# Two attention blocks, forward and backward: the DMA issues of GpSimd moved onto SyncE's queue in a written order

## The chip, the core and the metric

One core of a Trainium2 chip. The metric is the device time of one execution in microseconds (us); of several runs the median is given. Engines: PE (TensorE matmuls), PEld (its weight loads), DVE (VectorE), ACT (ScalarE), POOL (GpSimd), SP (SyncE, which only issues transfers here).

## The reference

Two independent attention blocks A and B with cached keys and values, their outputs side by side, and the gradients of all ten inputs for a given `grad_out`. All arrays are bf16. For each block:

```
B, Sq, D = 8, 96, 640;  H, Sk, Dh = 32, 512, 128
q = (x @ wq) in heads                     # [8, 32, 96, 128]
scores = einsum("bhqd,bhkd->bhqk", q, k_cache) * Dh**-0.5
p = softmax(scores)
o = einsum("bhqk,bhkd->bhqd", p, v_cache)
out = o in rows [8, 96, 4096] @ wo        # [8, 96, 640]
# and by the chain rule: dx, dk_cache, dv_cache, dwq, dwo
```

The bulk of the traffic is k_cache and v_cache (33.6 MB each per block) and their gradients, as large.

## The kernel before, in words

The kernel is one stream of ticks. A tick is one batch element b of one head h of one block; a head has 8 ticks, a block 256, and block B follows A without a break. Each step of the work is a Python closure handed to an emitter with a tick and a slot (`em.add(tick, slot, fn)`, L21); the emitter sorts by tick, then slot, and calls them, so that the order of the program is that of the sorted list. A scheduler behind it may move instructions of an engine past each other; those wrapped in `pinned` (L111) stay in program order on their engine. Slots (L51) put transfers at LOAD = 0, the first of a tick, and the attention steps between 5 and 54; head work is at 90, group work at 95.

For a tick ct the steps lie at fixed distances (`OFF`, L45): K is loaded 5 ticks ahead, V 3 ahead; K is transposed either by PE (`c_s1`, L285) or, for every second pair of batch elements of most heads, by a DMA transpose (`c_xt`, L275) 3 ahead; V is always transposed by a DMA transpose at ct itself. All of these are on SP. Loads and transposes are for a pair of batch elements: 256 KB, `NB = 2`. Then come the scores S (L298), their maximum on DVE (L300), the exponential on ACT (L310), the normalised P on POOL (L329) at ct+3, the transposed P (L365) and dV (L389, evicted by ACT at L392) at ct+4, O (L359) and the product O x dO on POOL (L407) at ct+5, dP and its row term dl (L417, L419) and dS on DVE (L421) at ct+6, the transposed dS (L346) and dK (L432, evicted by ACT at L435) at ct+7, dQ (L340) at ct+8. L340 is the last that reads K, L417 the last that reads the transposed V. K has 7 buffers, V 5, the transposed V 4, the transposed K 2.

Per head there is also: loading wq for two heads (`pA`, L190; 320 KB) and wo (`pA2`, L199; 160 KB) some ten ticks ahead, their transposes, the projections of Q and dO (L243), and behind the head the gradients dwo (`qB`, L470) and dwq for two heads (`qD`, L490). Every five or six heads (a group) the output rows and dx rows are accumulated in SBUF (`gU`, L512); at the last group they are written out. At the change of block, x and grad_out of block B are loaded in 12 row tiles `ld_tmp` (L118) and transposed on PE (L134), and loaded again in natural layout (L144).

Transfers are issued from two engines:
- SP: K and V loads, DMA transposes, x and grad_out. Only the `ld_tmp` loads are pinned; the order of the rest is the scheduler's.
- POOL, between its products: the stores of dV and dK (`c_st`, L398; 256 KB each, one of each for a pair, at the end of a tick: slot 54.3), the weights (slot 54.6), dwo (L474) and dwq (L496) as soon as their last part is evicted, and the output and dx rows of block A (L543). For the last head of B and its rows, SP issues these.

The eviction buffers of dV and dK are three each; dwo and dwq have one each.

Of the kernel before, what the change touches and what calls it, by code (L numbers as in the profile page):

```python
# [53 lines left out]
def build_block(tc, em, tick0, blk, x, kc, vc, wq, wo, g_all, out_all, dx, dk, dv, dwq, dwo, ident, ones, pools, HG=6, first=True, groups=None):  # L54
    nc = tc.nc
# [206 lines left out]
    def c_ld(h, b, n, bufs):  # L262
        def f():
            src = kc if n == "K" else vc
            X = kvp.tile([128, NB, KC, 128], BF16, name=n + "_sb", bufs=bufs)
            nc.sync.dma_start(X[:], src[b:b + NB, h].rearrange("b (p c) d -> p b c d", c=KC))
            for i in range(NB):
                st = CS.setdefault((blk, h, b + i), {})
                st[n + "_sb"], st[n + "_all"] = X[:, i], X
        return f  # L270

    def c_xt(h, b, name, bufs):
        def f():
            XT = kvp.tile([128, NB * KC, 128], BF16, name=name, bufs=bufs)
            nc.sync.dma_start_transpose(XT[:], CS[(blk, h, b)][name[0] + "_all"][:].rearrange("p a c d -> p (a c d)"))  # L275
# [119 lines left out]
    def c_st(h, b, which):  # L395
        def f():
            dst = dv if which == "v" else dk
            pinned(nc.gpsimd.dma_start(dst[b - 1:b + 1, h].rearrange("b (p c) d -> p b (c d)", c=KC), SB.pop((blk, h, b // 2, which))[:]))  # L398
        return f
# [59 lines left out]
    def qB(h, di):  # L459
        def f():  # L460
            st = HS[(blk, h)]
            Onat = st["Onat"]
            if "dwo_sb" not in st:
                st["dwo_sb"] = hd.tile([128, D], BF16, name="dwo_sb", bufs=1)
                st["dwo_n"] = 0
            dwo_sb = st["dwo_sb"]
# [4 lines left out]
            evac(EV["qB%d" % di], dwo_sb[:, c0:c0 + w], w_ps[:])  # L471
            st["dwo_n"] += 1
            if st["dwo_n"] == len(wsplits):
                (nc.gpsimd if first or h < H - 1 else nc.sync).dma_start(dwo[h * 128:(h + 1) * 128, :], dwo_sb[:])  # L474
        return f

    def qD(h, c_lo, c_hi):
        def f():
            st = HS[(blk, h)]
            dQnat = st["dQnat"]  # L480
            if "dwq_sb" not in st:
                st["dwq_sb"] = hd.tile([128, DC, 256], BF16, name="dwq_sb", bufs=1)
                st["dwq_n"] = 0
            dwq_sb = st["dwq_sb"]
# [7 lines left out]
            evac(EV["qD"], dwq_sb[:, c_lo:c_hi, :].rearrange("p a b -> p (a b)"), w_ps[:, 0:ncn * 256], scale)  # L492
            st["dwq_n"] += ncn
            if st["dwq_n"] == DC:
                with nc.allow_non_contiguous_dma(reason="dwq slice of two heads"):
                    (nc.gpsimd if first or h < H - 1 else nc.sync).dma_start(dwq_v[:, :, (h - 1) * 128:(h + 1) * 128], dwq_sb[:])  # L496
        return f
# [3 lines left out]
    def gU(g, which, t, gi):  # L501
        def f():
# [39 lines left out]
            if gi == len(gsplits) - 1:  # L542
                (nc.gpsimd if first else nc.sync).dma_start(dst_flat[t * 128:(t + 1) * 128, :], ob)  # L543
        return f
# [7 lines left out]
    for g in range(NG):  # L552
        h0 = GH0[g]
        for hh in range(groups[g]):
            h = h0 + hh
            c0t = tick0 + h * B
            if not (first and h == 0):
                em.add(c0t + HK["pA"], 54.6, pA(h))
                em.add(c0t + HK["pA2"], 54.6, pA2(h))
            em.add(c0t + HK["pB"], SL_HEAD, pB(h))  # L560
# [11 lines left out]
            for b in range(B):  # L572
# [169 lines left out]
```

## Time and profile before

| | before |
|---|---|
| runs | 1705.34, 1693.32, 1706.98 us |
| median | 1705.34 us |
| span of the profiled execution | 1699.8 us, granted PE clock 0.998 |
| time of the profiled execution | not told by the page; the span is 5.5 us under the median |
| PE, DVE, ACT, POOL busy | 99, 78, 83, 61% of the span |
| DMA issues | 927 on SP (378 of them transposes), 713 on POOL |
| moved by DMA | 423 MB, mean 249 GB/s |

How to read it: the span is from the first to the last instruction of one execution. A matmul's end is modelled, and matmuls overlap, so PE's busy share tells where it stood still and not how near it is to its peak. A row of a wait view says which instruction waited, what ended the wait (`<-`), and then the total in us, the number of waits and the longest. In rows of instructions `x256 | 195.0, 762 | 9.1` is count, busy us, mean ns of one, and the engine's idle us before them. `SPq` is SP's instruction queue. The time to landing of a DMA runs from its issue to the last of its bytes.

### The profile page before, as it was taken

Reading aid. Unit: us, or ns where it says so; the run is one execution under the profiler, and the core shown is the slowest. Engines: PE = TensorE matmul, PEld = TensorE weight load, DVE = VectorE, ACT = ScalarE, POOL = GpSimd, SP = SyncE. Lnnn points to the kernel's source line nnn. Section 1 sums busy time; section 2 is a strip of 40 time slices with the busy share of each in tenths; the row PEclk is TensorE's granted clock in tenths of the full one; section 3 lists DMA queues with packets and bytes.
Section 4 is the critical chain, followed back from the end, with each engine's and each line's share of the span. In section 5 each row is a group of like instructions: output and inputs, shape, how many; then the busy total and the mean of one; then the engine's idle time right before and its main releaser. Section 6 shows DMA issues by size and latency. Waiting matters only on the chain.

```text
span 1699.8 us, 56567 instructions
## 1 busy us (share of the span) xinstructions
PE 1675.7 (99%) x22024; PEld 1343.8 (79%) x22024; DVE 1329.8 (78%) x3052; ACT 1405.2 (83%) x3518; POOL 1040.3 (61%) x1747
## 2 busy tenths in 40 slices
PE   8999999999999999999999999999999999999999
PEld 7877778778778778777778877887788778778876
DVE  6887678878788878787778876787788778878877
ACT  6998889869869869878768998897799679878975
POOL 3676567646647647656566764675576557656754
PEclk9999999999999999999999999999999999999999
DMA  9999999999999999999999999999899989999994
GB/s 256 252 259 250 258 225 260 262 242 243 262 221 252 268 238 259 225 251 237 281 256 269 273 270 248 238 289 248 218 261 276 237 221 261 281 217 240 263 247 141
DMA packets 600429, 423.05 MB, mean 249 GB/s; under 512 B 419360, under 2 KB 557984, under 8 KB 600160
## 3 DMA queue, kind: packets, MB, share of 16 engines
q1 hardware_dynamic: 546576, 242.08, 72.2%
q0 software_dynamic: 53584, 177.35, 32.7%
q8 instruction: 173, 2.83, 0.7%
q14 instruction: 96, 0.79, 0.2%
HBM read 161.09 MB, written 159.12 MB: 188 GB/s over the span
## 4 chain that ended last, share of the span: by engine, by line
PE 89%; DMA 4%; ACT 3%; issue 1%; DVE 1%; POOL 0%; SPq 0%; DVEq 0%; ACTq 0%; POOLq 0%
PE q_ps L243 12%; PE o_ps L512 12%; PE dwo_ps L470 6%; PE dV_ps L389 6%; PE dK_ps L432 6%; PE S_ps L298 6%; PE dP_ps L417 6%; PE dwq_ps L490 6%; PE x_ps L340 5%; PE x_ps L365 5%; PE dst_ps L346 5%; PE x_ps L359 5%; PE kT_ps L285 3%; PE n_ps L258 3%; PE nat_ps L455 2%; DMA VT<-V_sb 1%
## 5 line engine op out<-in xcount | busy, mean ns | idle before, releaser
L329 POOL TENSOR_SCALAR P_sb<-E_sb,rinv 96x512 bf16<-96x512 bf16 x512 | 352.6, 689 | 567.8 <-DVE rinv L320 559.2
L310 ACT ACTIVATE E_sb<-S_ps,negm 96x512 bf16<-96x512 f32 x512 | 351.0, 686 | 187.6 <-DVE negm L300 181.9
L421 DVE SCALAR_TENSOR_TENSOR dS_sb<-dP_ps,dl_ps,P_sb 96x512 bf16<-96x512 f32 x512 | 382.1, 746 | 60.9 <-PE dl_ps L419 54.6
L300 DVE TENSOR_REDUCE negm<-S_ps 96x1 f32<-96x512 f32 x512 | 347.6, 679 | 50.9 <-PE S_ps L298 46.6
L435 ACT ACTIVATE dK_sb<-dK_ps 128x512 bf16<-128x512 f32 x512 | 302.1, 590 | 63.4 <-PE dK_ps L432 56.5
L392 ACT ACTIVATE dV_sb<-dV_ps 128x512 bf16<-128x512 f32 x512 | 311.6, 609 | 0.0
L378 ACT ACTIVATE PT_sb<-x_ps 128x384 bf16<-128x384 bf16 x512 | 253.1, 494 | 0.0
L512 PEld LDWEIGHTS <-OD 128*128 128x128 bf16 x1536 | 132.2, 98 | 100.4 <-issue 1.0
L398 POOL DMA_DIRECT2D out_dram<-dV_sb x256 | 194.9, 761 | 11.8 <-issue 8.6
L398 POOL DMA_DIRECT2D out_dram<-dK_sb x256 | 195.0, 762 | 9.1 <-issue 4.4
L389 PE MATMUL dV_ps<-dOnat_h,P_sb 96*128 96x128 bf16 x2048 | 198.2, 219 | 0.8 <-DVE dOnat_h L160 0.6
L417 PE MATMUL dP_ps<-VT,dOT_h 128*96 128x512 bf16 x512 | 195.4, 382 | 3.0 <-DMA VT<-V_sb 3.0
L432 PE MATMUL dK_ps<-Qnat_h,dS_sb 96*128 96x128 bf16 x2048 | 198.1, 219 | 0.1
L407 POOL TENSOR_TENSOR prod<-OD,dOT_h 128x96 bf16<-128x96 bf16 x512 | 184.2, 360 | 13.8 <-ACT OD L375 12.6
L348 DVE COPY dST_sb<-dst_ps 128x384 bf16<-128x384 bf16 x512 | 177.1, 346 | 10.5 <-PE dst_ps L346 10.3
L365 PE MATMUL x_ps<-ident,P_sb 96*128 96x96 bf16 x2048 | 172.0, 205 | 0.8 <-POOL P_sb L329 0.3
L359 PE MATMUL x_ps<-PT_sb,V_sb 128*128 128x96 bf16 x2048 | 172.3, 206 | 0.2 <-ACT PT_sb L378 0.2
L346 PE MATMUL dst_ps<-ident,dS_sb 96*128 96x96 bf16 x2048 | 172.3, 206 | 0.2 <-DVE dS_sb L421 0.2
L340 PE MATMUL x_ps<-dST_sb,K_sb 128*128 128x96 bf16 x2048 | 171.0, 206 | 1.3 <-ACT dK_sb L435 0.8
L375 ACT ACTIVATE OD<-x_ps 128x192 bf16<-128x192 f32 (+1 forms) x515 | 167.9, 326 | 3.9 <-PE x_ps L340 3.9
L320 DVE RECIPROCAL rinv<-rowsum 96x1 f32<-96x1 f32 x512 | 79.9, 156 | 106.0 <-ACT E_sb L310 100.4
L340 PEld LDWEIGHTS <-K_sb 128*128 128x128 bf16 x2048 | 131.1, 98 | 25.1 <-issue 1.6
(84 smaller groups left out, 3744.4 us busy)
## 6 DMA issues: line engine op xcount, KB each, us to landing
out_dram<-dV_sb POOLq DMA_DIRECT2D x256, 256.0 KB, 5.2
out_dram<-dK_sb POOLq DMA_DIRECT2D x256, 256.0 KB, 5.3
K_sb<-in_A_k_cache_dram SPq DMA_DIRECT2D x128, 256.0 KB, 5.3
V_sb<-in_A_v_cache_dram SPq DMA_DIRECT2D x128, 256.0 KB, 5.2
K_sb<-in_B_k_cache_dram SPq DMA_DIRECT2D x128, 256.0 KB, 5.0
V_sb<-in_B_v_cache_dram SPq DMA_DIRECT2D x128, 256.0 KB, 4.9
out_dram<-dwo_sb POOLq DMA_DIRECT2D x63, 160.0 KB, 4.8
out_dram<-dwq_sb POOLq DMA_DIRECT2D x31, 320.0 KB, 6.1
```

The source lines that it names most:

```text
L300: nc.vector.tensor_reduce(negm[:], S_ps[:], axis=AX.X, op=ALU.max, negate=True)
L310: nc.scalar.activation(E_sb[:], st["S_ps"][:], ACT.Exp, bias=st["negm"][:], scale=1.0, accum_out=rowsum[:])
L329: pinned(nc.gpsimd.tensor_scalar(P_sb[:], st["E_sb"][:], st["rinv"][:], 0.0, op0=ALU.mult, op1=ALU.add))
L340: nc.tensor.matmul(dQT_ps, st["K_sb"][:, c, :], st["dST_sb"][:, c * Sq:(c + 1) * Sq], start=(c == 0), stop=(c == KC - 1))
L389: nc.tensor.matmul(dV_ps[:, c * 128:(c + 1) * 128], P_sb[:, c * 128:(c + 1) * 128], hs["dOnat_h"][:, b * 128:(b + 1) * 128], start=True, s ...
L392: nc.scalar.activation(SB[(blk, h, b // 2, "v")][:, b % 2], dV_ps[:], ACT.Identity, scale=1.0)
L398: pinned(nc.gpsimd.dma_start(dst[b - 1:b + 1, h].rearrange("b (p c) d -> p b (c d)", c=KC), SB.pop((blk, h, b // 2, which))[:]))
L417: nc.tensor.matmul(dP_ps[:], hs["dOT_h"][:, tok], st["VT"], start=True, stop=True)
L421: nc.vector.scalar_tensor_tensor(dS_sb[:], dP_ps[:], dl_ps[:, 0:1], st["P_sb"][:], op0=ALU.subtract, op1=ALU.mult)
L432: nc.tensor.matmul(dK_ps[:, c * 128:(c + 1) * 128], dS_sb[:, c * 128:(c + 1) * 128], hs["Qnat_h"][:, b * 128:(b + 1) * 128], start=True, s ...
L435: nc.scalar.activation(SB[(blk, h, b // 2, "k")][:, b % 2], dK_ps[:], ACT.Identity, scale=1.0)
L512: nc.tensor.matmul(o_ps[:], src[:, t * 128:(t + 1) * 128], rhs, start=(hh == 0), stop=(hh == groups[g] - 1))
```

## The change

All 713 issues on POOL move to SP. There the K and V loads, the DMA transposes, the stores and the weights are now pinned, in a written order; the first weights and the loads in natural layout are not. Within a tick SP's order is: loads (slot 0), transposes (1), the stores of dV and dK (1.5), dwo, dwq and rows (1.6), weights (1.7). The stores of dV and dK keep their tick, one behind the eviction, but stand at the beginning of that tick and no longer at its end. The stores of dwo, dwq, the output rows and dx rows become steps of their own (`qB_st`, `qD_st`, `gU_st`), one tick behind their last product. The weights keep their ticks, ten and nine ahead of their head. The first wo load goes to SP too, and is not pinned.

In the built program PE, DVE and ACT have the same sequence of instructions as before, and POOL the same but for the DMAs. For a pair SP's order becomes V load, K load, K transpose (every second pair), dK store, V transpose, dV store.

```diff
@@ pA, pA2
-                        pinned(nc.gpsimd.dma_start(wq_p[:], wq_v[:, :, h * 128:(h + 2) * 128]))
+                        pinned(nc.sync.dma_start(wq_p[:], wq_v[:, :, h * 128:(h + 2) * 128]))
...
-            ld = nc.gpsimd.dma_start(wo_h[:], wo[h * 128:(h + 1) * 128, :])
+            ld = nc.sync.dma_start(wo_h[:], wo[h * 128:(h + 1) * 128, :])
@@ c_ld, c_xt
-            nc.sync.dma_start(X[:], src[b:b + NB, h].rearrange("b (p c) d -> p b c d", c=KC))
+            pinned(nc.sync.dma_start(X[:], src[b:b + NB, h].rearrange("b (p c) d -> p b c d", c=KC)))
...
-            nc.sync.dma_start_transpose(XT[:], CS[(blk, h, b)][name[0] + "_all"][:].rearrange("p a c d -> p (a c d)"))
+            pinned(nc.sync.dma_start_transpose(XT[:], CS[(blk, h, b)][name[0] + "_all"][:].rearrange("p a c d -> p (a c d)")))
@@ c_st
-            pinned(nc.gpsimd.dma_start(dst[b - 1:b + 1, h].rearrange("b (p c) d -> p b (c d)", c=KC), SB.pop((blk, h, b // 2, which))[:]))
+            pinned(nc.sync.dma_start(dst[b - 1:b + 1, h].rearrange("b (p c) d -> p b (c d)", c=KC), SB.pop((blk, h, b // 2, which))[:]))
@@ qB, qD, gU
+    def qB_st(h):
+        def f():
+            pinned(nc.sync.dma_start(dwo[h * 128:(h + 1) * 128, :], HS[(blk, h)]["dwo_sb"][:]))
...
+    def qD_st(h):
+        def f():
+            with nc.allow_non_contiguous_dma(reason="dwq slice of two heads"):
+                pinned(nc.sync.dma_start(dwq_v[:, :, (h - 1) * 128:(h + 1) * 128], HS[(blk, h)]["dwq_sb"][:]))
...
+    def gU_st(which, t):
+        def f():
+            dst_flat = out_flat if which == 0 else dx_flat
+            pinned(nc.sync.dma_start(dst_flat[t * 128:(t + 1) * 128, :], S.pop(("ob", which, t))))
@@ build_block
-                em.add(c0t + HK["pA"], 54.6, pA(h))
-                em.add(c0t + HK["pA2"], 54.6, pA2(h))
+                em.add(c0t + HK["pA"], SLOTS["LOAD"] + 1.7, pA(h))
+                em.add(c0t + HK["pA2"], SLOTS["LOAD"] + 1.7, pA2(h))
...
-                    em.add(ct + OFF["s4"] + 1, 54.3, c_st(h, b, "v"))
-                    em.add(ct + OFF["s7"] + 1, 54.3, c_st(h, b, "k"))
+                    em.add(ct + OFF["s4"] + 1, SLOTS["LOAD"] + 1.5, c_st(h, b, "v"))
+                    em.add(ct + OFF["s7"] + 1, SLOTS["LOAD"] + 1.5, c_st(h, b, "k"))
...
+            em.add(c0t + hk["qB"][-1] + 1, SLOTS["LOAD"] + 1.6, qB_st(h))
...
+            if h % 2 == 1:
+                em.add(c0t + hk["qD"][-1][0] + 1, SLOTS["LOAD"] + 1.6, qD_st(h))
...
+            if g == NG - 1 and gi == len(gsplits) - 1:
+                em.add(tk + 1, SLOTS["LOAD"] + 1.6, gU_st(which, t))
```

More of the change, by code (lines that the diff above doesn't have):

```diff
@@ L464, in f @@
                 st["dwo_sb"] = hd.tile([128, D], BF16, name="dwo_sb", bufs=1)
-                st["dwo_n"] = 0
             dwo_sb = st["dwo_sb"]
@@ L471, in f @@
             evac(EV["qB%d" % di], dwo_sb[:, c0:c0 + w], w_ps[:])
-            st["dwo_n"] += 1
-            if st["dwo_n"] == len(wsplits):
-                (nc.gpsimd if first or h < H - 1 else nc.sync).dma_start(dwo[h * 128:(h + 1) * 128, :], dwo_sb[:])
+        return f
+    def qB_st(h):
+        def f():
+            pinned(nc.sync.dma_start(dwo[h * 128:(h + 1) * 128, :], HS[(blk, h)]["dwo_sb"][:]))
         return f
@@ L482, in f @@
                 st["dwq_sb"] = hd.tile([128, DC, 256], BF16, name="dwq_sb", bufs=1)
-                st["dwq_n"] = 0
             dwq_sb = st["dwq_sb"]
@@ L492, in f @@
             evac(EV["qD"], dwq_sb[:, c_lo:c_hi, :].rearrange("p a b -> p (a b)"), w_ps[:, 0:ncn * 256], scale)
[L493 to L496, printed above, removed]
+        return f
+    def qD_st(h):
+        def f():
+            with nc.allow_non_contiguous_dma(reason="dwq slice of two heads"):
+                pinned(nc.sync.dma_start(dwq_v[:, :, (h - 1) * 128:(h + 1) * 128], HS[(blk, h)]["dwq_sb"][:]))
         return f
@@ L542, in f @@
             if gi == len(gsplits) - 1:
-                (nc.gpsimd if first else nc.sync).dma_start(dst_flat[t * 128:(t + 1) * 128, :], ob)
+                S[("ob", which, t)] = ob
+        return f
+    def gU_st(which, t):
+        def f():
+            dst_flat = out_flat if which == 0 else dx_flat
+            pinned(nc.sync.dma_start(dst_flat[t * 128:(t + 1) * 128, :], S.pop(("ob", which, t))))
         return f
```

## The prediction

> **What bounds the kernel now.** I read four views in this order: the page's busy times and chain, PE's waits, the DMA queues, and the rows of the engines that issue DMAs.
>
> ```profile
> PE 1675.7 (99%) x22024; PEld 1343.8 (79%) x22024; DVE 1329.8 (78%) x3052; ACT 1405.2 (83%) x3518; POOL 1040.3 (61%) x1747
> ...
> PE 89%; DMA 4%; ACT 3%; issue 1%; DVE 1%; POOL 0%; SPq 0%; DVEq 0%; ACTq 0%; POOLq 0%
> ```
>
> PE has 99% of the span and 89% of the chain that ended last. Busy time is no peak, so I checked it by the starts of successive matmuls in the trace: 42 ns apart at 96 columns, 56 at 128, 110 at 256, 135 at 320, 216 at 512, that is columns/2.4 + 2 ns. Over all 22,024 matmuls this sums to 1618 us. Of the span of 1699.8 us only 82 us are left, 5 of them before the first and after the last matmul, and some 20 at the hand-over behind each of the 512 one-column dl_ps matmuls. The change leaves PE's order untouched (the built programs of both kernels have the same sequence on PE, DVE and ACT). So what it can win is the part of PE's stalls that DMAs cause. PE's waits, and ACT's one:
>
> ```profile
> PE dP_ps L417 <- DMA VT<-V_sb: 3.0, 2, 2.4
> PE tp_ps L134 <- DMA ld_tmp<-in_grad_out_dram: 2.7, 1, 2.7
> PE S_ps L298 <- DMA KT<-K_sb: 2.1, 1, 2.1
> PE kT_ps L285 <- ACT dK_sb L435: 1.6, 1, 1.6
> ...
> PE tp_ps L134 <- DMA ld_tmp<-in_B_x_dram: 0.9, 1, 0.9
> ```
>
> ```profile
> ACT dK_sb L435 <- DMA out_dram<-dK_sb: 3.1, 2, 1.8
> ```
>
> Each row: us in total, times, longest. They are few and long: late transposes of V and K, late loads for the change of block, and twice an eviction of dK that has no free buffer since an earlier dK store has not landed. A long one costs twice, by the clock:
>
> ```profile
> 826.00:829.00 3.00, 0.26 (x3) 0.16 (x3) 0.00 (x0) 0.86 (x2) 0.88 (x2) 1.00 1.02 367
> 829.00:832.00 3.00, 3.00 (x35) 2.67 (x34) 1.75 (x5) 1.86 (x5) 0.81 (x2) 0.62 1.30 283
> ```
>
> In the windows view (us; PE, PEld, DVE, ACT, POOL busy; granted clock; DMA share; GB/s) PE stands still at 826 to 829 us, and then runs at a mean clock of 0.62. The clock records show half rate for 3.4 us, twice in the span: after this stall and after the one at 123 us.
>
> Why are those transfers late? SP stands in its own way:
>
> ```profile
> SPq L275 <- DMA K_sb<-in_A_k_cache_dram: 169.4, 57, 9.0
> SPq L275 <- DMA K_sb<-in_B_k_cache_dram: 152.0, 61, 4.8
> ```
>
> 118 of the 122 K transposes wait on SP for the load of their K: in the trace 119 of them are issued only two places behind it. The wait is 2.7 us on average, and all loads and transposes behind it wait too; then they leave in a burst.
>
> ```profile
> q1 hardware_dynamic: 546576, 242.08, 72.2%
> q0 software_dynamic: 53584, 177.35, 32.7%
> ```
>
> These are packets, MB, and packet time as a share of 16 engines: q1 is SP's queue, q0 POOL's. Together 105%: with both at work, packets wait for each other.
>
> **The change part by part.** The tick is 3.24 us (first L417 matmul at 23.3, last at 1679.5 us, 511 steps), a pair of ticks 6.48 us.
>
> POOL loses 713 issues (256+256 stores of dV and dK, 63 dwo, 31 dwq, 64 wo, 31 wq, 12 output rows).
>
> ```profile
> L398 POOL DMA_DIRECT2D out_dram<-dK_sb x256 | 195.0, 762 | 9.1 <-issue 4.4
> L398 POOL DMA_DIRECT2D out_dram<-dV_sb x256 | 194.9, 761 | 11.8 <-issue 8.6
> ```
>
> With the smaller groups 525 us of its 1040 go. POOL is not the bound: it waits 559 us for rinv. Ten PE stalls end with P_sb; only at 278.0 and 516.4 us did a POOL issue directly precede the late P_sb, 0.28 and 0.24 us. Gain 0.5 us (bounds 0 and all ten, 2.5).
>
> SP gains these 713. Its prices:
>
> ```profile
> L266 SPq DMA_DIRECT2D K_sb<-in_A_k_cache_dram x128: 367/478/1639, 2.4 to 814.3; - x128
> ```
>
> ```profile
> L275 SPq DMA_TRANSPOSE VT<-V_sb x256: 1231/1440/6143, 12.2 to 1656.9; - x128
> ```
>
> (ns, min/median/max.) No 256 KB store is issued by SP before; the nearest row is the K load, equal in bytes. By the minima, 1262 plain DMAs x 0.37 + 378 transposes x 1.23 = 932 us, 55% of the span. By the means of the trace (362.7 us / 549 = 0.66 and 600.1 / 378 = 1.59) 1434 us, 84%, or 5.6 of the 6.48 us of a pair. Both fit. I take nearer the minima, since the long ones stand in bursts behind other transfers.
>
> The waits that come in. The order on SP is now, for a pair, V load, K load, K transpose (every second pair), dK store, V transpose, dV store. The K load waits for PE's L340 matmul of its tick (seven buffers), as before. A dK store waits for ACT's eviction of the tick before, and behind it on SP stand the V transpose, the dV store and the next loads. In the timeline a dK matmul at 802.15 us is evicted by 803.75, and the next tick's L340, which the K load ahead of the store needs, starts at 804.77: the product is there a microsecond early. The dV store has a tick of its own in the same way. Cost nothing; if ACT ran more than that late, the V transposes would be late next, with 11.9 us between landing and use in the median of the trace (5% under 2.7). In return the K transpose now stands 6 or 8 places behind its K load in 116 of 122 cases: the 321 us of waits above go, and the bursts.
>
> In both built programs eight landing semaphores go round on SP's queue, so each DMA waits for the eighth before it to land. There were 927 DMAs, 3.6 a pair, eight of them 14.3 us; now 1640, 6.4 a pair, eight of them 8.1 us. Landings took 5.2 us (K loads) to 6.1 (V transposes) in the median, 8.5 and 10.2 at 95%. So this wait is new in the tail; a landing late by 2 us is covered by the 11.9.
>
> The DMA engines. In the packet records the median 256-byte packet of a transpose takes 18 ns (mean 31), 1,024 bytes of a load 46 (53), and POOL's packets of 4,096 bytes 165 (204). By the medians all traffic takes 1281 us of 16 engines, 75%. On SP's queue the stores leave in 1,024, 1,280 and 512-byte packets (46, 55, 27 ns): 377 + 61 + 67 = 505 us in place of 445, in all 1341 us, 79%: 5.24 us of a pair. The other end, with the means (72.2% of the span, and 505 x 53/46 = 577), is 1804 us, 106%. I take the medians, as the means hold the wait for the other queue's packet, which is no more.
>
> Two rules of the Trainium skill, page "DMA: Bandwidth & Descriptors", speak against this. "Why small descriptors are slow (HBM only)" puts about 3 cycles on each packet: as an estimate from it, four of 1,024 bytes cost 7% more than one of 4,096, where the rows have 12% (4 x 46 against 165); by it the stores take some 30 us more of DMA time, by the rows 60, and both fit into the idle fifth. "Queues, rings and completion order" says that an engine goes round its queues packet by packet; in one queue a load cannot pass a store any more. The 31 ns against 18 above agree with the first half. By the rule a load behind a dK and a dV store lands later by 2 x 256 packets x 46 ns / 16 = 1.5 us, and by the old turn-taking by about as much, so nothing in the sum.
>
> The stalls that go, from the starts of matmuls: V transposes 2.54 and 0.74 (at 122.7 and 711.0 us), K transposes 2.36, loads for the change of block 2.91 and 1.03, dK buffers 0.93 and 1.81 (787.7, 793.6): 12.3 us. With them half-rate clock for 2 x 3.4 us, 3.4 us of work. Lost at the start: the first wo load now goes ahead of the second part of x on SP, one issue of 0.45 us; PE waits there (0.41 us at 7.4), so 0.5 (0 to 1.0). At the end SP issues the last rows now and before; their order hardly moves: 0.
>
> Sum: 12.3 + 3.4 + 0.5 - 0.5 = 15.7 us off the 1699.8 us span, 1684.1. The page does not tell the profiled execution's time; the three runs have 1693.3 to 1707.0, median 1705.3, 5.5 above the span. Against the median: 1689.6 us. Ends: half of it, if the change of block still stalls (12 ld_tmp loads besides the rest in six pairs, 5.24 + 12 x 0.35 / 6 = 5.9 us of 6.48, so little room): 1697. And 1682, if nothing lies around the span in the run that the median stands for (1684.1) and all ten P_sb stalls go (2.0 more).
>
> **The rivals.**
> A, stalls trade places: the waits above go, but landings through one queue are late as often, or the new eighth-landing wait holds a transpose. For it: lone stalls of 1 to 3 us decide all, and 5% of V transposes had under 2.7 us. Against it: the K transposes' waits go. Time: 1705.
> B, slower: eight landings pace the queue. At 6.4 DMAs a pair it decides once the mean landing passes 8.1 us. Priced at the K loads' 95% row, 8.48 us: 6.4 x 8.48 / 8 = 6.78 us a pair, 0.30 x 256 = 77 us, about 1782. For it: the 106% end of the DMA sum (which alone would give 1804 + 5.5). Against it: medians of 5.2 to 6.1 us under two queues in bursts, and on a quiet queue at the end 160 KB rows landed in 1.8.
> C, no effect, since the transfers were hidden: 1700 to 1707. Against it: PE's wait rows name them. It is in A's chance.
>
> **How the numbers follow.** Gain 0.68, A and C 0.15, B or another clog of the one queue 0.17. About 1% is what a measurement of this kernel can tell from no change: 1688.3. Gain runs from 1682 to 1697 and is cut there: 0.34 under, 0.34 above. So faster 0.34, same 0.49, slower 0.17. The range goes from 1682 to 1712, beyond A by the spread of the runs; B is left out.
>
> **What would show it.** Right: PE's waits on VT, KT, ld_tmp and on dK_sb gone; no half-rate clock after the start; POOL near 515 us busy; SP's waits for K_sb near nothing; q1 alone, at 80 to 90%, landings under 6 us. Wrong: landings over 8 us, SP waits on a DMA eight back, q1 near 100%, or PE stalls in every pair.

## The result, and the profile after

| | before | after |
|---|---|---|
| runs side by side | 1705.34, 1693.32, 1706.98, 1694.21 us | 1684.34, 1684.02, 1684.36, 1684.57 us |
| median | 1699.78 us | 1684.35 us |
| ratio, 95% interval | | 0.9885 (0.9839 to 0.9931) |
| span of the profiled execution | 1699.8 us | 1682.6 us (time 1684.34 us) |
| POOL busy | 61% | 31% |
| DMA issues on SP | 927 | 1640 |

The changed kernel is faster by 1.15% (interval 0.7 to 1.6%; the two medians of the table alone differ by 0.9%). In later comparisons the kernel before had medians of 1701.5 to 1709.4 us, and in one of them single runs from 1699.9 to 1715.9, while the four runs of the changed kernel agree within 0.6 us: what went is a loss that differed from run to run. Executions over 1.5% above the fastest of the same kernel are left out of all times and ratios here (three of the ten of `e13_all_pool`, a few of the kernel before).

The page of the changed kernel: busy times, and the chain that ended last, where DMA had 4% before.

```profile
PE 1669.0 (99%) x22024; PEld 1340.4 (80%) x22024; DVE 1328.7 (79%) x3052; ACT 1403.1 (83%) x3518; POOL 527.6 (31%) x1034
...
PE 92%; ACT 4%; issue 1%; DVE 1%; DMA 1%; POOL 0%; SPq 0%; DVEq 0%; ACTq 0%; POOLq 0%
```

PE's waits in the changed kernel (us in total, times, longest): the first two rows. The waits for VT, KT, `ld_tmp` and for a free dK buffer are gone; the only DMA that PE still waits for is x at the start.

```profile
PE tp_ps L134 <- DMA x_nat<-in_A_x_dram: 1.5, 2, 1.2
PE warm_ps L671 <- DVE warm L658: 1.1, 1, 1.1
```

SP's waits: those for loads of K, on top of the list before (169.4 and 152.0 us), are gone but for 0.2 us. What is left on top is a load of K or V (L266) that waits for PE to free its buffer, which is as early as it can go.

```profile
SPq L266 <- PE dK_ps L432: 281.7, 157, 4.6
SPq L275 <- PE S_ps L298: 63.1, 50, 3.3
```

The change of block in the windows view (columns as before): the stall that stood at 826 to 829 us in the kernel before comes here at about 812, and is none; PE is busy throughout at full clock.

```profile
808.00:811.00 3.00, 3.00 (x49) 2.71 (x48) 2.76 (x8) 2.85 (x8) 1.02 (x2) 1.00 1.30 321
811.00:814.00 3.00, 3.00 (x41) 2.19 (x38) 2.34 (x7) 2.66 (x8) 1.02 (x2) 1.00 1.02 329
```

The DMA queues: one in place of two, with the same 419.43 MB.

```profile
q1 hardware_dynamic: 746528, 419.43, 101.2%
```

Since PE's order is the same in both kernels, the same matmul can be found in both traces, and the difference of its start tells where the time came from. It grows by 2.6 us at the V transpose at 125 us (time in the kernel before), 2.1 at a K transpose (159), 0.3 and 0.2 at two late P_sb (278, 516), 1.0 at a V transpose (712), 1.2 and 2.2 at the two dK buffers (788, 795), and 0.1, 0.7 and 2.9 around the loads for the change of block (807, 813, 829), less what is given back right behind: 13.3 us of stalls. Behind the stalls at 125 and 829 us it grows by 1.5 and 1.2 us more while the clock before is at half rate: 2.7 us. At the start it grows by 1.3 us; there the clock reached full rate at 5.9 us after and at 10.5 before. Together that is 17.3 us, as much as the spans differ.

### The profile page after: what moved, and what is told of

It is laid out like the page before. It is cut to its first block, busy times and chain, and to the rows that moved or that the text cites. A ratio compares the mean times of both kernels' runs of the same rounds, so it can differ in the third digit from the quotient of the medians.

```text
span 1682.6 us, 57184 instructions
## 1 busy us (share of the span) xinstructions
PE 1669.0 (99%) x22024; PEld 1340.4 (80%) x22024; DVE 1328.7 (79%) x3052; ACT 1403.1 (83%) x3518; POOL 527.6 (31%) x1034
## 3 DMA queue, kind: packets, MB, share of 16 engines
q1 hardware_dynamic: 746528, 419.43, 101.2%
## 4 chain that ended last, share of the span: by engine, by line
PE 92%; ACT 4%; issue 1%; DVE 1%; DMA 1%; POOL 0%; SPq 0%; DVEq 0%; ACTq 0%; POOLq 0%
PE q_ps L243 12%; PE o_ps L514 12%; PE dwo_ps L469 6%; PE dK_ps L432 6%; PE dV_ps L389 6%; PE dwq_ps L490 6%; PE S_ps L298 6%; PE dP_ps L417 6%; PE x_ps L340 5%; PE x_ps L365 5%; PE dst_ps L346 5%; PE x_ps L359 5%; PE kT_ps L285 3%; PE n_ps L258 3%; PE nat_ps L455 2%
## 5 line engine op out<-in xcount | busy, mean ns | idle before, releaser
L435 ACT ACTIVATE dK_sb<-dK_ps 128x512 bf16<-128x512 f32 x512 | 301.6, 589 | 56.7 <-PE dK_ps L432 53.8
L417 PE MATMUL dP_ps<-VT,dOT_h 128*96 128x512 bf16 x512 | 195.2, 381 | 0.0
L407 POOL TENSOR_TENSOR prod<-OD,dOT_h 128x96 bf16<-128x96 bf16 x512 | 185.7, 363 | 12.7 <-ACT OD L375 11.8
L365 PE MATMUL x_ps<-ident,P_sb 96*128 96x96 bf16 x2048 | 171.7, 205 | 0.6 <-POOL P_sb L329 0.3
L243 PE MATMUL q_ps<-gT,woT_h 128*128 128x512 bf16 (+1 forms) x640 | 136.9, 325 | 1.2 <-ACT gT L157 0.6
L469 PE MATMUL dwo_ps<-g_nat,Onat 128*128 128x320 bf16 x768 | 135.2, 298 | 1.6 <-ACT E_sb L310 0.2
```

The source lines that it names most:

```text
L243: nc.tensor.matmul(q_ps[:], lhs(c), rhsT[:, c, t0:t0 + w], start=(c == 0), stop=(c == DC - 1))
L417: nc.tensor.matmul(dP_ps[:], hs["dOT_h"][:, tok], st["VT"], start=True, stop=True)
L435: nc.scalar.activation(SB[(blk, h, b // 2, "k")][:, b % 2], dK_ps[:], ACT.Identity, scale=1.0)
```

## The experiments

For each kernel I also worked out, over all DMA issues of its trace, the time from issue to landing. In the kernel before it is 5.53 us in the mean, 10.9 at the 99th percentile and 14.9 at most; in the changed kernel 4.10, 6.4 and 7.8. The theory of the forecast (SP stands in its own way behind K loads, so the order is what helps) stands against a first rival (it is the second queue), and later against a second one (the DMA engines are nearly full, and this is why a second queue hurts).

**Order alone, and queue alone.** `e1_order_alone` takes the kernel before and pins loads and transposes into the written order; the 713 transfers stay on POOL. `e2_queue_alone` takes the kernel before, moves the 713 to SP, and leaves the places to the scheduler.

```diff
# e1: kernel before
-            nc.sync.dma_start(X[:], ...)
+            pinned(nc.sync.dma_start(X[:], ...))
-            nc.sync.dma_start_transpose(XT[:], ...)
+            pinned(nc.sync.dma_start_transpose(XT[:], ...))
# e2: kernel before; likewise for wq, wo, dwo, dwq and the rows
-            pinned(nc.gpsimd.dma_start(dst[b - 1:b + 1, h]...
+            pinned(nc.sync.dma_start(dst[b - 1:b + 1, h]...
```

> The kernel before with only the K and V loads and the DMA transposes pinned, so that SP's order becomes V, K, K transpose, V transpose with the K transpose a pair (4 places) behind its load; all stores and weights stay on POOL. Theory 1 (SP's order made the stalls): PE's waits on DMAs fall from 12 us to under 2 us, SP's waits for K_sb from 321 us to under 40, time 1684 to 1689 us. Theory 2 (two queues sharing the engines made the transfers late): landings stay at 5 to 6 us, PE stalls of 1 to 3 us stay, time 1694 to 1706.

> The kernel before with all of POOL's DMAs issued by SP, but nothing more pinned and no store moved to another tick: the scheduler sets the places, the K transpose 4 to 7 places behind its load, loads and stores wherever they fall. Theory 1 (order): stores that wait for a product, or K transposes too near their loads, hold up SP, PE stalls stay, time 1690 to 1706. Theory 2 (queue): landings near 4 us, no PE wait on a DMA, time 1684 to 1687.

Measured: e1 1738.89 us, ratio 1.0184 (1.0145 to 1.0223), above the ranges of both theories. e2 1684.76 us, ratio 0.9879 (0.9864 to 0.9894), as theory 2 wanted. The whole gain is there with the one queue and without the written order; the order without the queue is slower than the kernel before. In e1 the waits of SP for K loads fall from 321 us to 146, and PE waits more all the same. PE's and SP's waits in e1:

```profile
PE S_ps L298 <- DMA KT<-K_sb: 30.9, 10, 8.3
```

```profile
SPq L275 <- DMA K_sb<-in_A_k_cache_dram: 78.0, 39, 4.9
SPq L275 <- DMA K_sb<-in_B_k_cache_dram: 67.9, 37, 4.7
```

The ten K transposes of the first row took 6.6 to 18.8 us to land (4.6 in the mean of the changed kernel). Eight of them had been issued 5.2 to 18.4 us before PE wanted them: these were slow transfers. The two with the longest waits (8.3 and 6.4 us) were slow, 12.1 and 9.2 us, and also issued late, 3.9 and 2.9 us ahead. Landings of all DMAs in e1: 6.32 us in the mean, 13.5 at the 99th percentile, 18.8 at most. SP's waits for K loads, the forecast's cause, do not explain this run.

**The same wait in one queue.** `e3_kt_close` is the changed kernel with the K transpose two or three places behind its K load.

```diff
-OFF = dict(ldk=-5, ldv=-3, kt=-3, ...
+OFF = dict(ldk=-5, ldv=-3, kt=-4, ...
-                        em.add(ct + OFF["kt"], SLOTS["LOAD"] + 1, c_xt(h, b, "KT", 2))
+                        em.add(ct + OFF["kt"], SLOTS["LOAD"] + 0.9, c_xt(h, b, "KT", 2))
```

> The changed kernel with the K transpose one tick earlier, so that it stands 2 or 3 places behind its K load on SP as before the change, all else on SP in the written order. Theory 1 (order): SP waits for K_sb 200 us or more again, V transposes land later, lone PE stalls come back, time 1688 to 1700. Theory 2 (queue): SP's waits come back but landings stay near 4 us and no PE stall follows, time within 1 us of 1684.4.

Measured: 1794.79 us, ratio 1.0522 (1.0500 to 1.0543), far above the ranges of both theories. SP's, ACT's and PE's waits:

```profile
SPq L275 <- DMA K_sb<-in_A_k_cache_dram: 185.9, 60, 4.8
SPq L275 <- DMA K_sb<-in_B_k_cache_dram: 182.9, 62, 4.6
```

```profile
ACT dK_sb L435 <- DMA out_dram<-dK_sb: 81.5, 54, 3.9
```

```profile
PE x_ps L340 <- ACT dK_sb L435: 17.9, 13, 3.3
PE S_ps L298 <- ACT dK_sb L435: 16.3, 11, 3.0
```

The 369 us are about the 321 of the kernel before, but now 713 more DMAs stand behind them. SP falls behind: the wait that was its longest in the changed kernel, a load held back until PE frees its buffer, shrinks from 281.7 us to this:

```profile
SPq L266 <- PE dK_ps L432: 21.9, 34, 2.3
```

SP arrives when the buffer has long been free. So the stores leave late, their buffers come free late, ACT waits and PE waits for ACT. Landings are as short as in the changed kernel (4.17 us in the mean). So in the one queue a K transpose must stand some places behind its load; in e2 the scheduler happened to put most of them four to seven places behind.

**The first weights.** `e6_first_wo_pool` puts the first wo load back on POOL.

```diff
-            ld = nc.sync.dma_start(wo_h[:], ...
+            ld = (nc.gpsimd if first and h == 0 else nc.sync).dma_start(wo_h[:], ...
```

> The changed kernel with only the first wo load issued by POOL again, so that the second part of x goes out one place earlier on SP. The step of 0.9 us that the changed kernel loses against the one before at 7.4 to 7.9 us of the span should go: 1683.5 us, 0.9 under the changed kernel, if nothing else at the start follows it. If the start is paced by the weights or by the clock's first window, within 0.3 us of 1684.4.

Measured: 1684.49 us, ratio 0.9876 to the kernel before, as e2 has. No difference: that load costs nothing where it is.

**Which traffic on the second queue.** From the changed kernel, `e8_stores_pool` puts the 512 stores of dV and dK back on POOL, `e11_weights_pool` the 201 others, `e13_all_pool` all 713 (in e11 and e13 the last 14, which SP issued in the kernel before too, go to POOL with them), `e10_dv_pool` only dV, and `e9_dv_act` gives dV to ACT's hardware queue.

```diff
# e8; e10 and e9 have (nc.gpsimd or nc.scalar if which == "v" else nc.sync)
-            pinned(nc.sync.dma_start(dst[b - 1:b + 1, h]...
+            pinned(nc.gpsimd.dma_start(dst[b - 1:b + 1, h]...
# e11, likewise wo, dwo, dwq and the rows; e13 is e8 and e11
-                        pinned(nc.sync.dma_start(wq_p[:], ...
+                        pinned(nc.gpsimd.dma_start(wq_p[:], ...
```

> The changed kernel, with all 512 stores of dV and dK back on POOL's queue at the same ticks; loads, transposes, weights and output rows stay on SP in the written order. Theory Q (two queues lengthen each transfer, whatever the order): landings on SP go back to a mean over 5 us with a tail over 10 us (4.1 and 7.8 at most in the changed kernel), PE waits again for V, K or x transfers, 1697 to 1740 us. Rival O (the order on SP and its distances decide; the stores' queue does not matter as long as no transpose stands close behind its load): 1683 to 1688 us. Rival W (the weights and output rows, not the stores, were what disturbed): 1683 to 1688 us with landings near 4.2 us.

> The changed kernel, with the 256 dV stores issued by ACT on a hardware queue of its own; all else stays on SP. ACT gets 256 issues more, at about 0.4 to 0.5 us each some 115 us on an engine that is 83% busy: near 90%. Theory Q (any second queue): landings on SP between those of the changed kernel (mean 4.1 us) and of the kernel before (5.5), at least 4.6, some over 8 us. Rival S (only POOL's software queue does it): landings on SP stay at 4.0 to 4.3 us. Time: up to 1690 us if ACT's issues fit beside its work, 1700 to 1760 us if evictions come late behind them, and then PE waits for ACT, not for a DMA; the landings, not the time, tell Q from S.

> The changed kernel, with the 256 dV stores back on POOL's queue, the 256 dK stores on SP. The same bytes go through the second queue as in the run with dV on ACT's queue, so the two are compared by their landings. Theory Q: landings as there, at least 4.6 us in the mean, 1686 to 1710 us. Rival S (POOL's queue is special): landings longer than with ACT's queue by 0.4 us or more. Rival O: 1683 to 1688 us and landings near 4.2.

> The changed kernel, with the 201 weight loads, weight gradients and output rows back on POOL's queue, dV and dK stores on SP: the complement of the run that puts only the stores back (1688.8 us, landings on SP 4.5 us in the median for K loads). Theory Q (a second queue with any traffic lengthens the loads beside it, in proportion to its bytes): a third of those bytes, so K loads near 3.9 us and 1684 to 1688 us. Rival W (the bunched weights make the old stalls, not the steady stores): landings with a tail over 9 us, PE waits for V, K or x, 1690 to 1720 us.

> The changed kernel with its ticks and its order on SP, but all 713 stores, weight transfers and output rows back on POOL's queue (the two halves alone gave 1688.8 and 1689.6 us, landings 4.89 and 4.51 us in the mean against 4.10). If a second queue costs by its bytes, the halves add: 1693 to 1698 us, mean landing near 5.3 us. If they grow on each other, as the order alone with POOL's stores in the old places let one think (1738.9 us, 6.3 us): 1715 us or more, landings of 6 us with up to fifteen in flight.

Measured (landings of all DMAs of the profiled execution in us; that execution is not always near the median: it took 1695.53 us in e8, 1735.38 in e15; the last two rows are told below):

| kernel | MB on the second queue | mean | 99% | longest | median time, us | ratio (interval) |
|---|---|---|---|---|---|---|
| after | none | 4.10 | 6.4 | 7.8 | 1684.35 | 0.9885 (0.9839 to 0.9931) |
| e2 | none | 4.25 | 6.6 | 7.7 | 1684.76 | 0.9879 (0.9864 to 0.9894) |
| e10 | 67 | 4.81 | 7.6 | 10.3 | 1684.52 | 0.9895 (0.9865 to 0.9924) |
| e11 | 46 | 4.51 | 8.9 | 13.6 | 1689.60 | 0.9921 (0.9882 to 0.9961) |
| e9 | 67 (ACT's) | 4.58 | 7.3 | 8.2 | 1725.38 | 1.0132 (1.0100 to 1.0164) |
| e8 | 134 | 4.89 | 8.9 | 10.8 | 1688.78 | 0.9914 (0.9874 to 0.9953) |
| before | 177 | 5.53 | 10.9 | 14.9 | 1699.78 | 1 |
| e13 | 180 | 5.61 | 12.5 | 18.0 | 1723.84 | 1.0090 (1.0050 to 1.0130) |
| e1 | 177 | 6.32 | 13.5 | 18.8 | 1738.89 | 1.0184 (1.0145 to 1.0223) |
| e14 | 110 of 352 | 4.12 | 7.9 | 11.7 | 1687.24 | 0.9887 (0.9844 to 0.9931) |
| e15 | 180 | 5.77 | 12.0 | 15.8 | 1725.94 | 1.0095 (1.0060 to 1.0130) |

In all of these but e9 the time follows the 99th percentile more closely than the mean: nothing up to 7.6 us, 3 to 5 us at 8 to 9, 15 and more from 11 on. e10 and e8 hardly differ in the mean, and by 4 us in time. The halves (e8 and e11: 4.4 and 5.3 us) do not add up to the whole (e13: 39), which is what the second theory for e13 had. PE's longest wait in e13 is again for a DMA:

```profile
PE S_ps L298 <- DMA KT<-K_sb: 15.1, 6, 5.2
```

e13 is the changed kernel but for the queue of POOL's transfers, so here the queue alone makes the difference.

Theory Q's time ranges were missed by e8 (below 1697) and e10 (below 1686); its landings were met by e10 and nearly met by e8 (4.95 us on SP, over 5 wanted) and e9 (4.58, 4.6 wanted). e11 lies between its two theories: a tail to 13.6 us, as rival W had it, but a time just under W's 1690. e9 and e10 have the same bytes in the second queue, 4.58 and 4.81 us: 0.23 apart where the rival about POOL's queue wanted 0.4, so by these two executions most of it comes with any second queue. e9 itself took 1725.38 us for another reason, ACT's 256 more instructions; PE's first waits there are for ACT and not for a DMA:

```profile
PE nat_ps L455 <- ACT E_sb L310: 9.1, 22, 1.5
PE dK_ps L432 <- ACT dK_sb L435: 4.0, 8, 1.3
```

**Are the DMA engines full?** One more transfer per pair of ticks that nothing reads: `p1_pad_one` a K load of 256 KB on SP, `p3_pad_small` the same with 32 KB, `p4_pad_pool` the 256 KB on POOL; `p5_pad_sp_st` a store of 256 KB on SP, `p6_pad_pool_st` that store on POOL, `p7_pad_two` two stores on SP.

```diff
# p1 (p4: nc.gpsimd; p3: pad [128, 128] and kc[b, h, 0:128, :])
+            pad = kvp.tile([128, NB, KC, 128], BF16, name="pad", bufs=1)
+            pinned(nc.sync.dma_start(pad[:], kc[b:b + NB, h]...
# p5 (p6: nc.gpsimd; p7: a second one at ct + 1)
+            pinned(nc.sync.dma_start(PAD[i], S["g_nat"][:, 0:2, 0:512]))
# all
+                    em.add(ct, SLOTS["LOAD"] + 1.8, c_pad(h, b))
```

> The changed kernel with one more K load of 256 KB per pair of ticks on SP, into a buffer that nothing reads: 7.4 DMAs a pair in place of 6.4, and 0.74 us more of packet time a pair (5.24 + 0.74 = 5.98 of 6.48 us by the median packets). Forecast's view (landings near 4.1 us, by the medians the DMA engines have a fifth to spare, SP a quarter): 1684 to 1692 us, landings up to 5 us. Rival B of the forecast (the one queue is near its limit; by the mean packets its engines are over 100% busy): the extra 14% cannot be taken, PE waits in every pair, 1750 us or more.

> As the run with one more 256 KB load per pair (1744 us), but the load is of 32 KB, 128 packets of 256 bytes: the 256 extra issues on SP stay, seven eighths of the extra bytes go. If the 59 us that the padding cost came of SP's time to issue: near 1744 us still, at least 1720. If they came of the DMA engines' bytes and packets: 1684 to 1692 us. If of eight landings that pace the queue (7.4 DMAs a pair): over 1700 us, with eight DMAs in flight in over 5% of the time.

> As the run with one more 256 KB load per pair (1744 us), but POOL issues it on its own queue: the bytes stay, SP's extra issues go. If the 59 us came of SP's time to issue: 1684 to 1700 us. If of the DMA engines (110% packet time): 1725 to 1760 us again. In between, both count.

> The changed kernel with one more store of 256 KB per pair on SP's queue; the same store on POOL's queue gave 1731.6 us. If the bytes set the time and SP's issues come on top (14 us by the small pad): 1735 to 1750 us, and mean landings shorter than the 5.08 us that the second queue gave. If the second queue costs more than SP's issues: 1715 to 1730 us.

> The changed kernel with one more store of 256 KB per pair on POOL's queue, from a tile that lies still into memory that nothing reads, so that POOL does not wait for its one buffer as it did in the run with the padded load (whose PE then waited 35 us for P_sb). If the DMA engines' work costs the time (45 of the 59 us of the padded load on SP, less 14 that the small pad cost): 1715 to 1745 us. If SP's issues did: up to 1700 us.

> The changed kernel with two more stores of 256 KB per pair on SP's queue, 8.4 DMAs and some 31% more bytes. It measures what the DMA engines take at most. If they were already full with one pad per pair (280 GB/s over the span): the bytes set the time, 550 MB / 280 = 1960 us. If they take the 313 GB/s of the busiest twentieth of that run's 20 us windows: 1757 us or more. If eight landings paced the queue: eight in flight nearly always.

Measured: p1 1744.09 us (ratio 1.0240, 1.0206 to 1.0273), p3 1698.70 (0.9976, 0.9945 to 1.0006), p4 1758.28 (1.0340, 1.0265 to 1.0416), p5 1750.14 (1.0235, 1.0182 to 1.0287), p6 1731.63 (1.0144, 1.0102 to 1.0186), p7 1862.35 (1.0913, 1.0865 to 1.0961).

My forecast's view, an idle fifth, had p1 at 1684 to 1692 and has fallen; rival B's 1750 or more was not reached either, and p3 lies between its ranges. Against the changed kernel p5 costs 66 us. The same bytes without SP's issues (p6) cost 47, one more issue with an eighth of the bytes (p3) 14 (by the ratios to the kernel before, which was run beside each of them: 60, 44 and 16): the bytes are the larger part, SP's queue the smaller. p4 does not count, since its one buffer made POOL wait, and PE with it:

```profile
POOL pad L275 <- DMA pad<-in_A_k_cache_dram: 167.0, 78, 6.1
```

```profile
PE x_ps L371 <- POOL P_sb L335: 35.4, 39, 2.7
```

(The padded kernels have a few lines more, so their line numbers are shifted: L371 is L365 of the changed kernel, L447 its L435.) In p7 the DMA row of the page (packet time as a share of the 16 engines, in tenths, 40 slices) has a 9 in nearly every slice, and the rate beneath it lies near 300 GB/s throughout:

```profile
DMA  9999999999999999999999999999999999999995
GB/s 296 302 292 308 295 296 294 305 304 288 294 293 293 304 309 285 297 289 305 318 259 313 309 308 292 305 301 310 304 292 305 312 292 303 311 316 296 306 308 179
```

In the changed kernel the DMA row is nearly the same, so it does not tell whether the engines are full; but the rate swings between 195 and 301 GB/s (the last slice apart):

```profile
DMA  9999899989989989979999999999899899989984
GB/s 270 267 296 278 198 249 284 258 203 259 272 208 282 276 195 273 281 195 268 301 259 281 297 254 220 250 283 246 218 257 294 216 229 285 270 197 252 284 219 135
```

So it already runs at p7's rate for stretches and has room only between them. In total, by estimate: p7's two stores bring 127,744 packets of 1,024 bytes with a mean of 48 ns, 383 us of 16 engines. Even if the engines were full for all of p7's 1863 us, the rest, the changed kernel's own work, would be 1480 us, 88% of its span; or 1522 us, 90%, if these packets overlap as p7's packets do in all (112% of its span, so 383 / 1.12 = 342 us). That is an upper end, since SP was near its limit too in p7: 1648 us in DMA instructions, and the wait for a free buffer, 281.7 us in the changed kernel, down to this:

```profile
SPq L266 <- PE dK_ps L444: 19.7, 31, 4.4
```

Landings in p7 are 4.51 us in the mean, nearly as short as in e3, where SP was late. Whether the engines or SP set p7's time is not separated. The number of landings was no limit: eight were in flight in 0.5% of p7's time. The path by which the padded kernels lose is a late dK store, here in p7:

```profile
ACT dK_sb L447 <- DMA out_dram<-dK_sb: 148.6, 78, 5.3
```

**Fewer bytes, two queues.** `e14_half_stores` is the kernel before, each store of dV and dK writing one of its two sequences, so that half of dV and dK stays unwritten.

```diff
-            pinned(nc.gpsimd.dma_start(dst[b - 1:b + 1, h].rearrange("b (p c) d -> p b (c d)", c=KC), SB.pop(...)[:]))
+            pinned(nc.gpsimd.dma_start(dst[b, h].rearrange("(p c) d -> p (c d)", c=KC), SB.pop(...)[:, 1]))
```

> The kernel before (two queues, its own order), but each dV and dK store writes one of its two sequences: 67 MB of 419 are left out, the outputs of the other sequences stay unwritten. Number of DMAs, queues and order stay. If full DMA engines make the late landings and two queues only spread them: 1684 to 1690 us, mean landing under 4.8 us. If the two queues as such do it, whatever the load: within 6 us of the kernel before, landings still 5.2 us or more, SP waits for K_sb as before.

Measured: 1687.24 us, mean landing 4.12 us, in the ranges of the theory of full engines, and 19 us under the kernel before of the same comparison (1706.41) with its queues and its order untouched. SP still waits for K loads:

```profile
SPq L275 <- DMA K_sb<-in_A_k_cache_dram: 75.6, 53, 4.7
SPq L275 <- DMA K_sb<-in_B_k_cache_dram: 74.6, 58, 3.5
```

That is 150 us in place of 321, and it costs at most the 3 us to the changed kernel. But the smaller stores also take the second queue from 177 MB to 110, and e14's tail (7.9 us) and time lie between those of e10 and e8, which have 67 and 134 MB there and 419 in all. So this run does not tell the load of all engines from the load of the second queue. For the whole load speaks that K loads land in 3.8 us in the median, as in the changed kernel (4.3 in e10, 4.5 in e8).

**The tick between product and store.** `e12_store_early` puts the stores at the end of their product's own tick.

```diff
-                    em.add(ct + OFF["s4"] + 1, SLOTS["LOAD"] + 1.5, c_st(h, b, "v"))
-                    em.add(ct + OFF["s7"] + 1, SLOTS["LOAD"] + 1.5, c_st(h, b, "k"))
+                    em.add(ct + OFF["s4"], 60, c_st(h, b, "v"))
+                    em.add(ct + OFF["s7"], 60, c_st(h, b, "k"))
```

> The changed kernel, with each store of dV and dK handed to SP's queue behind its own tick's loads and transposes, not in the next tick: it can stand ready before ACT has evicted the product, and the next V and K loads wait behind it. If SP's idle time (436 us of the span in the changed kernel, most of it ahead of K loads that wait for a buffer) covers that: 1684 to 1688 us, with new SP waits for ACT. If the tick between product and store carries the gain: PE waits for VT, 1695 us or more.

Measured: 1684.51 us, ratio 0.9894 (0.9855 to 0.9933), landings as in the changed kernel (4.03 us). SP waits for ACT, as expected, and nothing comes of it:

```profile
SPq L398 <- ACT dV_sb L392: 134.1, 126, 3.8
```

**Were SP's waits a brake that did good?** With two queues, e1 and e13 were slower than the kernel before although SP waited less for K loads (146 and 76 us). `e15_close_pool` is e13 with the K transpose two places behind its load again.

```diff
# e13, and
-OFF = dict(ldk=-5, ldv=-3, kt=-3, ...
+OFF = dict(ldk=-5, ldv=-3, kt=-4, ...
-                        em.add(ct + OFF["kt"], SLOTS["LOAD"] + 1, c_xt(h, b, "KT", 2))
+                        em.add(ct + OFF["kt"], SLOTS["LOAD"] + 1.1, c_xt(h, b, "KT", 2))
```

> The run with all 713 DMAs back on POOL (1728.5 us, landings 5.61 us in the mean, up to fourteen in flight), but with SP's order as the scheduler had it in the kernel before: the K transpose two places behind its K load, so that SP stops at each for the load to land. If those stops hold SP back from filling full DMA engines further, that is if the wait that the forecast took for the cause was a brake that did good: 1698 to 1712 us, SP waits for K_sb of 300 us or more, fewer than twelve in flight. If the stops only lose time: 1735 us or more.

Measured: 1725.94 us against 1723.84 of e13 (1728.5 in the expectation, which counts all ten executions), in neither of the two ranges. SP waits 332 us for K loads again, in flight are up to fourteen as before:

```profile
SPq L275 <- DMA K_sb<-in_A_k_cache_dram: 169.0, 58, 6.5
SPq L275 <- DMA K_sb<-in_B_k_cache_dram: 162.8, 62, 7.6
```

With POOL's transfers where e13 has them, the waits neither help nor hurt. With them at their old places the order does matter: e1 differs from the kernel before by the pinned order alone, has 175 us less of these waits and is 33 us slower. Whether the waits are a brake there stays open. The kernel before is 17 us faster than e15 (1709.36 in the same comparison), with the same order on SP and nearly the same transfers on POOL. What is left is the places of POOL's transfers, within the tick and, for dwo, dwq and the rows, one tick later; that wasn't tried by itself.

## Why the prediction was right or wrong

**The number.** 1689.6 forecast, 1684.35 measured, inside the range; but "within 1%" was called likelier than "faster", and it is faster by 1.15%. Two terms of the sum were mis-sized. First, "the three runs have 1693.3 to 1707.0, median 1705.3, 5.5 above the span". In the later traces time and span differ by 1.7 us (1684.34 and 1682.6; in e13 1721.62 and 1719.9). So the profiled execution of before took about 1701.5, and the rest of the 5.5 is the distance of that execution from the median of runs whose stalls differ; the change removes it with the stalls, and I carried it over as if it were fixed. Second, the sum of 15.7 us, measured 17.3: stalls 12.8 against 12.3 (P_sb apart, 0.5 as forecast), clock 2.7 against 3.4, start a gain of 1.3 against a loss of 0.5. e6 shows that the first wo load costs nothing; whether the earlier clock at the start is the change's doing stays open. With 1.7 in place of 5.5 the same sum gives 1685.8, which is 1.1% under the median then known, below the 1688.3 that the prediction took as its line.

**The cause.** Which stalls would go, and that the half-rate clock goes with them, was right, row by row. Why they stood there, "SP stands in its own way", was the step that failed for the greater part. Seven transfers were late behind the stalls of the kernel before. Five of them had been issued 7.8 to 14.3 us before they were wanted and took 9.7 to 14.9 us to land, longer than any of the changed kernel (7.8): slow transfers. The other two are the K transpose at 159 us and the grad_out tile at 829 us, issued 4.5 and 3.7 us ahead, with landings of 6.5 and 6.4 us. Here SP did stand in its own way, as its queue in the kernel before shows (start, us):

```profile
146.54 2.25 SPq L275 DMA_TRANSPOSE VT<-V_sb  x1
152.24 1.29 SPq L275 DMA_TRANSPOSE KT<-K_sb  x1
```

```profile
816.00 2.70 SPq L275 DMA_TRANSPOSE VT<-V_sb  x1
821.10 1.23 SPq L275 DMA_TRANSPOSE KT<-K_sb  x1
822.42 1.39 SPq L118 DMA_DIRECT2D ld_tmp<-in_grad_out_dram  x1
```

Between each V transpose and the K transpose SP stood still for 3.4 and 2.4 us, until the K load had landed. The two waits of PE that followed are 4.8 of the 11.8 us that PE and ACT waited for the seven. But these two K loads took 7.5 and 6.8 us where the changed kernel has 3.9 in the mean, so slow transfers lie behind this too. The runs agree: e1 removes half of SP's waits for K loads and is slower, e14 keeps half of them and is within 3 us of the changed kernel, e15 restores them all and is as e13.

What the runs show in its place is the second queue. e13, the changed kernel with POOL's transfers back on POOL's queue, is 39 us slower; e8, e10 and e11 are parts of it. With 419 MB the 99th percentile of the landings is 7.3 to 13.5 us with two queues, by what stands on the second, and 6.3 to 6.6 with one. Why a second queue lengthens them stays open: that together they nearly fill the DMA engines fits the p runs and e14, but no run separates it.

**The DMA engines.** "I take the medians, as the means hold the wait for the other queue's packet, which is no more" is the step that failed here. In the one queue the 256-byte packets still have a median of 18 ns and a mean of 29 (31 before), and about half a per cent of them last over 1 us and hold a quarter of their time, before and after (24.9 and 25.3%). So q1 stands at 101.2%, not at 80 to 90; "q1 near 100%" was named as a sign of being wrong, and it came with the gain. By the estimate from p7 the load is at most some 90%, between the medians' 79% and the means' 106%; the idle fifth may be as little as a tenth, and it is unevenly spread.

**SP.** "Both fit" holds for the order as written: 1243 us in DMA instructions, 74%, between my 55 and 84%. It needed the K transpose well behind its load (six or eight places as written, mostly four to seven in e2), which the forecast had as a gain and not as a condition: e3, 110 us slower than the changed kernel, is what the one queue gives without it, a slower case that the rivals had only as "another clog of the one queue". The dK store that finds its product "a microsecond early" was right and, by e12, not even needed.

**Eight landings.** The price (8.1 us a pair) stands, and landings of 4.1 us stayed well under it: eight are in flight for 0.3% of the time. Rival B's mechanism is far from deciding; but its other support, the full engines, was nearer than the 0.17 said: 16% more bytes decide (p5).

**Turn-taking.** The forecast put the rule of "Queues, rings and completion order" (the Trainium skill, page "DMA: Bandwidth & Descriptors") at nothing in the sum. Loads through one queue land 1.5 us sooner (3.8 against 5.3 for K in A), not equally late. The "31 ns against 18" that was said to agree with it is no support, since the one queue has 29 against 18. That the engines go round the queues by packets would fit the longer tails; no run here separates it from other ways in which two queues could disturb each other, so it stays argued. The same page's "Rules for kernel authors" says that spreading DMAs over issuing engines buys no bandwidth and only saves issue time. p5 against p6 has such a saving (18.5 us, 15 by the ratios, with SP at 85% and 83% of the span in DMA instructions), and e8, e11 and e13 have what it can cost.

**POOL.** 527.6 us busy against "near 515"; P_sb's part of the gain was 0.5 us. Right.

## What to carry to other kernels

Where the trace shows late transfers, compare the landing times (99th percentile, not the mean) before blaming the issuing engine's waits: a wait there costs only what stands behind it, some 2 us in e15 against e13, where SP spends 57% of the span on its DMAs, and 110 us in e3, where stores and loads queue up behind it. For each late transfer, set its time to landing beside how long before its use it was issued: that tells a slow transfer from a late start. Where the traffic is as dense as here (249 GB/s), try it on one queue, in an order in which no instruction waits for a transfer issued just ahead of it, and test the slack by adding a transfer that nobody reads. If single runs spread by more than the time around the span, that spread may be part of what can be won.

## What the runs showed of the hardware

- The same 419 MB at about the same rate (244 to 251 GB/s) land in 4.0 to 4.3 us (mean) from one queue (the changed kernel, e2, e12) and in 5.5 to 6.3 with 177 to 180 MB of them on POOL's (the kernel before, e1, e13, e15); the 99th percentiles are 6.3 to 6.6 and 10.9 to 13.5.
- The queue's share of 16 engines can pass 100% with one queue alone: 101.2% at 249 GB/s, 111.3% at 295 GB/s in p7. So it counts packets that overlap, and is no measure of room.
- A 256 KB transfer holds SP for 0.37 us at least, a DMA transpose for 1.23; under load the means were 0.54 (all plain DMAs) and 1.50 (transposes) in the changed kernel, 0.58 and 2.17 in e1.
- In the kernel before, half-rate clock for 3.4 us followed the waits of PE of 2.4 and 2.7 us (rows L417 and L134); the one of 2.1 us (L298) had none behind it.
